# Linear attention beside an MLP: the second block pair's queries as chunk pairs of the seven-product loop

## The chip, the cores and the metric

The kernel runs on one core of a Trainium2 chip. The metric is the device time of one execution in microseconds (us), taken as the median of several runs; less is better.

## The reference

x is 2048 tokens by 512 channels, in float32. The kernel computes x + A(xn) + B(xn), where xn is x normalised over its channels:

```python
    qkv = (xn @ wqkv).reshape(B, S, 3, H, Dh)          # 32 heads of 16 channels
    phi = lambda t: jnp.where(t > 0, t + 1, jnp.exp(t)) + 1e-6
    pq, pk = phi(q), phi(k)
    kv = jnp.einsum("bhsd,bhse->bhde", pk, v)
    z = jnp.einsum("bhsd->bhd", pk)
    num = jnp.einsum("bhqd,bhde->bhqe", pq, kv)
    den = jnp.einsum("bhqd,bhd->bhq", pq, z)[..., None] + 1e-6
    A = (num / den) @ wo                               # heads side by side again
    h = relu(xn @ w1 + b1); B = (h * h) @ w2 + b2      # 1376 hidden features
```

## The kernel before, in words

TensorE takes its operands as rounded float32 (F32R). To keep accuracy, every operand is split into a high and a low part, and a product is three matmuls: high by high, high by low, low by high (`three`, L126). `split` (L116) makes the parts: ACT copies the high part out, DVE (or POOL) subtracts it for the low part.

The 2048 tokens are 16 tiles of 128 and four blocks of 512 (numbers 3, 2, 1, 0). The kernel goes over the tiles once for the keys and the sums of pk by xn (L693 to L736); then it goes over two pairs of blocks, blocks 3 and 2 with n = 0, blocks 1 and 0 with n = 1 (L837). x1 and x2 hold the two blocks' normalised tokens by channels, high and low parts; the tokens of blocks 1 and 0 wait in DRAM (xTd) until the first pair is done.

For each pair:

- *Queries* (`queries`, L404): one projection for each of the eight token tiles, 12 matmuls each, with tokens on the partitions; then phi (L368: ACT Relu, ACT Exp, DVE combine). For the second pair all eight stand at the start (L892 to L905), with the sums and the first weight splits between them.
- *Attention* (`attention`, L412): five DVE instructions for a token tile: multiply with z (zb, on all partitions), reduce over each head's 16 channels, add 1e-6, reciprocal, multiply. The denominators lie along the free dimension, so tokens stay on the partitions. `regroup_q` (L427) moves the finished 128-token tiles by DMA so that `attention_T` (L441) can turn them by 32x32 transposes on DVE to channels on the partitions, then makes high and low parts (aT). These are the stationary operands of `add_attention` (L509), whose moving operand m is the key-value matrix by wo.
- *The seven-product loop* (L970): the hidden features go in 11 chunks of 128; the last chunk, with 96, is done plainly (`plain_1`, L479). The other ten are five chunk pairs. A pair of chunks by two token blocks by two halves of the channels is a two by two by two product; it is computed with seven products instead of eight (the scheme of Strassen and Winograd). Each product (`product`, L485) is six matmuls of 128x512. The weights' sums S1 to S4 (`chunk_sums`, L743; splits into aop, L752 to L758) are made one iteration ahead, the tokens' sums T1 to T4 (`sums_of`, L775) once for each pair of blocks. The order in an iteration is fixed by hand: A (A11), B (A12), C (S1), the former pair's A22, S2 into A's bank, S4 into C's, S3 into A's. Between them ACT copies banks out (c11, t5, c12), DVE adds the other bank (L992, L978, L1046), and ACT applies Relu with the bias. c12 is copied after S2 and before S3 adds into the same bank. MLP sums (`mlp_2`, L493: 12 matmuls) of the first block stand between the products; with two of them, an iteration has 66 matmuls.
- *Second half* (L1082 to L1172): the first block's attention sums and output, then the second block's: nine MLP sums (index e), its attention sums, and the last two features. Here `wait_for` makes the hidden parts of the second block, which lie in r2, and `w2next` the parts of the w2 rows, three sums ahead. For the first pair this half also loads the next pair's tokens (L1096, L1124) and splits them (columns_todo), and splits wq for the next queries (`piece_q`, L171).

The program order is written out by hand (`manual_schedule`): every engine and every DMA queue takes its instructions in the order of the code. Nearly all DMAs go through SP's queue. Buffers come from pools with tags: "p" and "raw" have six slots of 128x512, "pair" five; a tile's slot waits for the last reader of the one before. TensorE has eight banks of PSUM: four for the products ("ps"), four for the block's output sums ("acc").

Of the kernel before, what the change touches and what calls it, by code (L numbers as in the profile page):

```python
# [18 lines left out]
def kernel(  # L19
# [130 lines left out]
    zb = keep.tile([P, D], F32, name="zb")  # L150
    eps = keep.tile([P, 1], F32, name="eps")
# [357 lines left out]
    def add_attention(acc, i, last=False):  # L509
        t = aT.pop(i)  # L510
        for j in range(NJ):
            three(acc[i % TB], [t[:, u, j * P:(j + 1) * P] for u in range(2)],
                  [m[u][:, j, :] for u in range(2)], False, last and j == NJ - 1)
# [226 lines left out]
    def load_1(n):  # L740
        return [raw_1(2 * n + k).rearrange("p (c n) -> p c n", c=2) for k in range(2)]
# [95 lines left out]
    for n in range(2):  # L837
        t1, t2 = NB - 1 - 2 * n, NB - 2 - 2 * n
        x1, x2 = xsb
        tag = "acc" if n else "ps"  # L840
        if n:

            o34 = [halves(xT[t])[1] for t in (t2, t1)]
            sums = sums_of(xT[t1], xT[t2], *o34)
        z = pair(f"w1z{n}") if n else None

        def small_chunk():
            t = raw_1(NF - 1)
            return lambda: split(z[:, 0], z[:, 1], t, "act", "dve")

        def first_split():
# [5 lines left out]
        def second_split(s12, s34):  # L857
# [4 lines left out]
        at1 = [lambda k=k: attention(t1 * TB + k) for k in range(TB)] + [lambda t=t1: regroup_q(t)]  # L862
        at1 += [lambda k=k: attentions_T(t1 * TB + k, t1 * TB + k + 1) for k in (0, 2)]
        at2 = [lambda k=k: attention(t2 * TB + k) for k in range(TB)]


        if n == 0:
            do(sums)
            queries(t1 * TB + 2)
            zs = small_chunk()  # L870
            w = load_1(0)
# [3 lines left out]
            z = pair("w1z0")  # L875
# [4 lines left out]
            ss = first_split()  # L880
# [5 lines left out]
            second_split(*ss)  # L886
            w2next = piece_2(NF - 1, 0)
            matrix(2)
        else:
            zs = small_chunk()  # L890
            w = load_1(0)
            for k in range(TB):  # L892
                queries(t1 * TB + k, tag)
                if k == 0:
                    zs()
                else:
                    do(sums)
            for k in range(TB):
                queries(t2 * TB + k, tag)
                if k == 0:  # L900
                    do(sums)
                if k == 1:
                    ss = first_split()
                if k == 2:
                    second_split(*ss)  # L905
# [5 lines left out]
        w = load_1(1)  # L911
# [58 lines left out]
        for p in range(NP + 1):  # L970
            fa, fb = 2 * p, 2 * p + 1
# [3 lines left out]
            if p < NP:  # L975
# [5 lines left out]
            if 0 < p < NP:  # L981
                chunk_split(1, 0, s34)
            if p:
                relu(r2[fb - 2], t5, fb - 2)
            if p == 1:
                next_2(2)
            if p < NP:
# [3 lines left out]
                high_2()  # L991
                nc.vector.tensor_tensor(out=c11, in0=B, in1=c11, op=OP.add)  # L992
                relu(c11, c11, fa)
            if p < NP:
                next_2(2 * p + 1)
# [3 lines left out]
            if p == NP:  # L999
                attention_places(*(("r1", "r3") if n else ("r2", "r0")))  # L1000
                do(at1)
                mlp_2(acc, fa - 2, s.pop(fa - 2))
            if p:
                product(before, A22b, [T[4][:, u] for u in range(2)], False, True)
                c21 = w512(f"c21_{n}_{p}", "p", 6)
                relu(c21, before, fb - 2)
            if p == NP:
                break
            t5 = t5_
            if p == 0:  # L1010
                T.update({k: tokens_sum(k, f"B{k - 3}") for k in (3, 4)})
# [6 lines left out]
            if p or n:  # L1018
                do(at1 if p < TB else at2)
            if p:  # L1020
                s[fb - 2] = hidden_2(f"s{n}_{fb - 2}", c21)
                mlp_2(acc, fa - 2, s.pop(fa - 2))
            else:
# [5 lines left out]
            s[fa] = hidden_2(f"s{n}_{fa}", c11)  # L1029
            if p + 1 < NP:  # L1030
# [3 lines left out]
            if p + 2 < NP:  # L1034
                w = load_1(p + 2)
            if p == NP - 1:
# [4 lines left out]
            if p + 1 < NP:  # L1041
                chunk_split(0, 1, s12)
            if p == NP - 1:
                do(at2)
            product(C, S4, [x[:, 2:] for x in x2], False, True)
            nc.vector.tensor_tensor(out=c12, in0=C, in1=c12, op=OP.add)  # L1046
            high_2()
            if p == 0:
                last_sums(4, difference_high)
            relu(r2[fa], c12, fa)  # L1050
            if p:
                next_2(2 * p + 2)
                mlp_2(acc, fb - 2, s.pop(fb - 2))
            else:
                for k in range(TB):
                    last_2(acc[k], k, sz, True, False)
                quarters_2(acc, sz)
            if p == TB - 1:
                do(at1)
                move(16)  # L1060
            product(A, S3, [T[3][:, u] for u in range(2)])
            if p == 2:
                load_res(t1)
            if p == 3:
# [18 lines left out]
        s1 = hidden_2(f"s{n}_{f}", c21)  # L1083
        for g in waiting[4:9]:
# [116 lines left out]
```

## Time and profile before

| | |
|---|---|
| median of 3 runs | 421.85 us (421.46 to 422.19) |
| the profiled execution's own time | 422.41 us |
| its span, first to last instruction | 420.7 us |
| busy: PE, DVE, ACT, POOL | 414.1, 304.9, 253.0, 55.2 us |
| mean granted TensorE clock | 0.999 |
| HBM read, written | 37.23 MB, 8.91 MB |

Engines: PE is TensorE (PEld its weight loads, which overlap), DVE VectorE, ACT ScalarE, POOL GpSimd, SP SyncE, whose queue issues DMAs. A profile row of a group gives line, engine, operation, output<-input, shapes, count, then busy us and mean ns of one, then the idle time of the engine before them and what released it. Rows of the chain and of the timeline begin with the start and the duration in us. Matmul records are pipelined and overlap: of two that follow each other the distance of the starts is the pace, not the duration.

### The profile page before, as it was taken

Reading aid. Unit: us, or ns where it says so; the run is one execution under the profiler, and the core shown is the slowest. Engines: PE = TensorE matmul, PEld = TensorE weight load, DVE = VectorE, ACT = ScalarE, POOL = GpSimd, SP = SyncE. Lnnn points to the kernel's source line nnn. Section 1 sums busy time; section 2 is a strip of 40 time slices with the busy share of each in tenths; the row PEclk is TensorE's granted clock in tenths of the full one; section 3 lists DMA queues with packets and bytes.
Section 4 is the critical chain, followed back from the end, with each engine's and each line's share of the span. In section 5 each row is a group of like instructions: output and inputs, shape, how many; then the busy total and the mean of one; then the engine's idle time right before and its main releaser. Section 6 shows DMA issues by size and latency. Waiting matters only on the chain.

```text
span 420.7 us, 5470 instructions
## 1 busy us (share of the span) xinstructions
PE 414.1 (98%) x1859; PEld 340.6 (81%) x1859; DVE 304.9 (72%) x555; ACT 253.0 (60%) x451; POOL 55.2 (13%) x78
## 2 busy tenths in 40 slices
PE   7999999999999999999999999999999999999996
PEld 6788888888887788888888887888788888888875
DVE  5995767786679987777579397586977667577293
ACT  5767777675467777565466371666677665546140
POOL 3231222220004000110000061001000200000240
PEclk9999999999999999999999999999999999999999
DMA  6885423800511322695026676501121784023742
GB/s 235 274 234 163 130 92 99 277 25 3 125 50 52 99 64 63 191 184 175 0 69 190 192 230 159 139 0 50 44 82 26 225 172 153 2 94 87 193 77 100
DMA packets 49485, 50.69 MB, mean 120 GB/s; under 512 B 8241, under 2 KB 33585, under 8 KB 49202
## 3 DMA queue, kind: packets, MB, share of 16 engines
q1 hardware_dynamic: 47154, 46.16, 36.4%
q0 software_dynamic: 2304, 4.20, 6.1%
q8 instruction: 14, 0.23, 0.3%
q14 instruction: 13, 0.11, 0.1%
HBM read 37.23 MB, written 8.91 MB: 110 GB/s over the span
## 4 chain that ended last, share of the span: by engine, by line
PE 96%; DMA 2%; DVE 1%; SPq 1%; issue 0%
PE acc L129 36%; PE b L489 23%; PE kx L398 10%; PE pq L379 10%; PE pk L379 9%; PE acc L500 2%; DMA x<-in_A_x_dram 2%; PE pz L129 1%; PE b L129 1%; PE pkv L820 1%; PE pm L129 1%; PE pt L318 0%; PE acc L507 0%; SPq L527 0%; SPq L157 0%; PE end L129 0%
## 5 line engine op out<-in xcount | busy, mean ns | idle before, releaser
L129 PE MATMUL acc<-w2r,s 128*128 128x512 f32 x477 | 112.8, 389 | 0.0
L129 PEld LDWEIGHTS acc<-w2r,s 128*128 128x128 f32 x477 | 89.5, 188 | 18.9 <-issue 0.2
L489 PE MATMUL b<-T,aop 128*128 128x512 f32 x240 | 59.9, 390 | 0.0
L489 PEld LDWEIGHTS b<-T,aop 128*128 128x128 f32 x240 | 44.8, 188 | 9.8 <-issue 0.5
L398 PE MATMUL kx<-pk,tok 128*128 128x512 f32 x192 | 46.8, 393 | 0.0
L398 PEld LDWEIGHTS kx<-pk,tok 128*128 128x128 f32 x192 | 35.6, 188 | 8.0 <-DVE pk L387 0.6
L956 POOL DMA_DIRECT2D res<-in_B_b_dram x16 | 14.1, 1067 | 150.5 <-DMA res<-in_A_x_dram 57.5
L121 DVE TENSOR_TENSOR w2r<-r,w2r 128x512 fp32r<-128x512 f32 (+2 forms) x35 | 25.4, 725 | 7.3 <-ACT w2r L110 7.2
L129 PE MATMUL acc<-mh,aTsr 128*128 128x512 f32 x96 | 30.6, 391 | 0.0
L118 POOL TENSOR_TENSOR tok<-xp,tok 128x512 fp32r<-128x512 f32 x16 | 21.7, 1363 | 54.8 <-ACT tok L110 54.8
L110 ACT ACTIVATE w2r<-r 128x512 fp32r<-128x512 f32 x32 | 20.0, 625 | 13.7 <-PE acc L129 11.3
L489 PE MATMUL b<-xs0h,aop 128*128 128x512 f32 x80 | 26.4, 391 | 0.0
L118 DVE TENSOR_TENSOR s<-c,s 128x512 fp32r<-128x512 f32 x20 | 13.8, 692 | 15.0 <-ACT s L110 14.9
L110 ACT ACTIVATE aop<-S 128x512 fp32r<-128x512 f32 x20 | 12.6, 629 | 16.1 <-DVE S L749 12.3
L374 DVE SCALAR_TENSOR_TENSOR q<-pq,q 128x512 f32<-128x512 f32 x16 | 11.0, 690 | 14.4 <-ACT q L372 14.4
L129 PEld LDWEIGHTS acc<-mh,aTsr 128*128 128x128 f32 x96 | 18.0, 188 | 4.0 <-issue 0.2
L370 ACT ACTIVATE q<-pq 128x512 f32<-128x512 f32 x16 | 9.4, 590 | 18.6 <-PE pq L379 18.5
L129 PE MATMUL acc<-ml,aTsr 128*128 128x512 f32 x48 | 18.7, 390 | 0.0
L964 DVE TENSOR_TENSOR res<-acc,res 128x512 f32<-128x512 f32 x16 | 11.0, 692 | 9.9 <-PE acc L129 6.6
L489 PEld LDWEIGHTS b<-xs0h,aop 128*128 128x128 f32 x80 | 15.0, 188 | 3.4 <-ACT rz L477 0.3
L303 DVE STREAM_TRANSPOSE at<-g 128x512 f32<-128x512 f32 x16 | 10.4, 689 | 7.9 <-DMA g<-q 7.9
L489 PE MATMUL b<-xs0l,aop 128*128 128x512 f32 x40 | 15.6, 390 | 0.0
(208 smaller groups left out, 854.9 us busy)
## 6 DMA issues: line engine op xcount, KB each, us to landing
r<-in_B_w_dram SPq DMA_DIRECT2D x49, 256.0 KB, 3.1
res<-in_A_x_dram SPq DMA_DIRECT2D x8, 512.0 KB, 5.8
res<-in_B_b_dram POOLq DMA_DIRECT2D x16, 256.0 KB, 5.3
g<-q SPq DMA_DIRECT2D x64, 64.0 KB, 2.5
out_dram<-res SPq DMA_DIRECT2D x15, 256.0 KB, 2.1
x<-in_A_x_dram SPq DMA_DIRECT2D x5, 512.0 KB, 6.0
via<-xp SPq DMA_DIRECT2D x5, 512.0 KB, 2.7
xg<-via SPq DMA_DIRECT2D x20, 128.0 KB, 2.9
```

The costliest lines, as they stand in the source:

```text
L110: nc.scalar.activation(o, i, AF.Copy, bias=bias)
L118: ENG[el].tensor_tensor(out=l, in0=src, in1=f32(h), op=OP.subtract)
L121: nc.vector.tensor_tensor(out=l, in0=src, in1=f32(h), op=OP.subtract)
L129: nc.tensor.matmul(ps, lhsT=a[u], rhs=b[v], start=first and n == 0, stop=last and n == 2)
L303: nc.vector.transpose(o.rearrange("p j (r t) -> p r j t", r=NJ), G.rearrange("p r (j c) -> p r j c", j=NJ))
L370: nc.scalar.activation(p, ps, AF.Relu, scale=-1.0)
L374: nc.vector.scalar_tensor_tensor(p, ps, 0.0, p, op0=OP.max, op1=OP.add)
L379: nc.tensor.matmul(ps, lhsT=cols(i)[u][:, j, slot(i)], rhs=w[v][:, j, :], start=first and n == 0, stop=last and n == len(steps) - 1)
L398: nc.tensor.matmul(kxp[c], lhsT=tok[i][:, u, c * P:(c + 1) * P], rhs=pk[i][:, v], start=i == 0 and (u, v) == first, stop=i == NT - 1 and ( ...
L489: nc.tensor.matmul(ps, lhsT=a[u][:, j * P:(j + 1) * P], rhs=b[v][:, j, :], start=first and j == 0 and n == 0, stop=last and j == 1 and n == 2,
L956: nc.gpsimd.dma_start(r[:, i], b2[None, :].partition_broadcast(P), accum_op=OP.add)
L964: nc.vector.tensor_tensor(out=r[:, a:z], in0=ps, in1=r[:, a:z], op=OP.add)
```

## The change

The second pair of blocks no longer projects its queries tile by tile. wq's 512 columns are treated as four more chunks of 128, two more chunk pairs of the loop, which for n = 1 runs over seven pairs in the order q, w, q, w, w, w, w. A query chunk comes out with channels on the partitions and 512 tokens along the free dimension, for both blocks, which is the layout that `add_attention` wants; so `regroup_q` and the turns go for this pair. The eight results (two blocks, four chunks) are called units here. The denominators need a sum over channels, now the partitions: `steps_of` weights the unit by z on ACT (a scale and a bias for each partition, from zc), turns the result in 32x32 blocks on DVE, reduces over each head's 16 channels, takes the reciprocal, and turns the quotients back with a read that repeats each one 16 times.

```diff
+    def phi_T(o, src):
+        e = w512("phi", "p", 6)
+        nc.scalar.activation(e, src, AF.Relu, scale=-1.0)
+        nc.scalar.activation(e, e, AF.Exp, scale=-1.0)
+        nc.vector.scalar_tensor_tensor(o, src, 0.0, e, op0=OP.max, op1=OP.add)
+
+    def steps_of(t, j, done=False, parts=False):
+        o = q[t][:, j]
+        tiles = []
+        blocks = lambda ap: ap.rearrange("p (r c) -> p r c", c=32)
+        heads_of = lambda ap: ap.rearrange("p (h d) -> p h d", h=H)
+        by_heads = lambda ap: ap.rearrange("p (r h) d -> p r h d", h=2)
+        def weighted():
+            pz = w512(f"pz{t}_{j}", "p", 6)
+            tiles.append(pz)
+            nc.scalar.activation(pz, o, AF.Identity, bias=zc[:, 1, j:j + 1], scale=zc[:, 0, j:j + 1])
+        def sums():
+            pt = w512(f"pt{t}_{j}", "p", 6)
+            den = small.tile([P, H], F32, name=f"dt{t}_{j}", tag="den")
+            nc.vector.transpose(blocks(pt), blocks(tiles[0]))
+            nc.vector.tensor_reduce(den, heads_of(pt), axis=AX.X, op=OP.add)
+            tiles.append(den)
+        def quotients():
+            pz, den = tiles
+            nc.vector.tensor_scalar(den, den, 1e-6, None, op0=OP.add)
+            nc.vector.reciprocal(den, den)
+            nc.vector.transpose(by_heads(heads_of(pz)), by_heads(den[:, :, None].to_broadcast([P, H, D // H])))
+        def divide():
+            nc.vector.scalar_tensor_tensor(o, o, 1e-6, tiles[0], op0=OP.add, op1=OP.mult)
+        def into_parts():
+            a = aT[t, j] = places.pop(0)
+            split(a[:, 0], a[:, 1], o, "act", "dve")
+        return [lambda: phi_T(o, o)][done:] + [weighted, sums, quotients, divide] + [into_parts][:parts]
...
+    def raw_q(f):
+        t = w512(f"rq_{f}", "raw", 6)
+        nc.sync.dma_start(t.rearrange("p (j n) -> p j n", j=NJ),
+                          wqkv[:, f * P:(f + 1) * P].rearrange("(j p) n -> p j n", j=NJ))
+        return t
...
+    def z_columns():
+        of_g = zd.rearrange("o (g j c) -> g c (o j)", g=NJ, j=NJ)
+        for g in range(NJ):
+            nc.sync.dma_start(zc[32 * g:32 * (g + 1), 0], of_g[g])
+        return lambda: nc.vector.tensor_scalar(zc[:, 1], zc[:, 0], 1e-6, None, op0=OP.mult)
...
+        order = [("w", k) for k in range(NP)]
         if n:
+            order[:1] = ("q", 0), ("w", 0), ("q", 1)
+        NO = len(order)
+        AT = ((0, 0, 0, 0, 0, 0, 0, 0, 0),
+              (0, 0, 0, 0, 1, 1, 0, 0, 0),
+              (2, 0, 0, 0, 1, 1, 0, 1, 0),
+              (2, 0, 0, 1, 1, 0, 1, 0, 1),
+              (2, 0, 1, 0, 0, 0, 1, 0, 1),
+              (0, 1, 0, 0, 0, 0, 0, 1, 0),
+              (1, 2, 1, 0, 0, 0, 2, 0, 0),
+              (1, 0, 1, 0, 1, 1, 0, 2, 3))
+        AE = (2, 1, 4, 2, 1, 3, 1, 7, 2, 3, 1)
```

AT says how many steps of the units are issued at each of nine places of an iteration (places in the order 7, 0, 1, 8, 2, 3, 4, 5, 6; `step` takes the first block's steps first), AE how many beside each MLP sum of the second half. In the loop:

```diff
-            if p:
-                nc.vector.tensor_tensor(out=t5, in0=before, in1=t5, op=OP.add)
+            if was:
+                nc.vector.tensor_tensor(out=t5 if was == "w" else q[t2][:, pb], in0=before, in1=t5, op=OP.add)
...
-                nc.vector.tensor_tensor(out=c11, in0=B, in1=c11, op=OP.add)
-                relu(c11, c11, fa)
+                nc.vector.tensor_tensor(out=c11 if kind == "w" else q[t1][:, fa], in0=B, in1=c11, op=OP.add)
+                if kind == "w":
+                    relu(c11, c11, fa)
+                else:
+                    steps[t1] += steps_of(t1, fa, parts=True)
...
+                else:
+                    phi_T(q[t1][:, pb], before)
+                    steps[t1] += steps_of(t1, pb, True, True)
...
-            if p == NP - 1:
+            if p > 1:
                 do(at2)
+            step(at_p[4])
             product(C, S4, [x[:, 2:] for x in x2], False, True)
...
+            def second_sums(f=pb, first=not was):
+                if first:
+                    for k in range(TB):
+                        last_2(acc[k], k, sz, True, False)
+                    quarters_2(acc, sz)
+                else:
+                    mlp_2(acc, f, s.pop(f))
+            if kind == "q":
+                put_off = second_sums
+            elif was != "q":
+                second_sums()
...
             product(A, S3, [T[3][:, u] for u in range(2)])
```

A put-off sum is issued in the next iteration, after the former pair's A22. `do(at2)` (an attention of the second block, n = 0) thus also stands in the third and fourth iterations. The z columns are loaded in the first pair's third iteration. For n = 1 the eight `queries` calls are gone: the small chunk's product follows the first pair's last sums at once.

The first pair's second half takes over what stood among the second pair's queries, and drops wq's pieces; both token loads move ahead of the w2 pieces:

```diff
+        prepare = []
+        if n == 0:
+            f1, f2 = (keep.tile([P, NJ, BT], F32, name=f"xT{t}", tag=f"xT{k}") for t, k in ((t1 - 2, t1), (t2 - 2, t2)))
+            nc.sync.dma_start(f1, xTd[t1 - 2])
+            nc.sync.dma_start(f2, xTd[t2 - 2])
+            o34 = halves(four("Tf1", "r0"))
...
+            prepare = [lambda x=x, f=f, j=j: columns(x, f, j) for j in range(NJ) for x, f in ((x1, f1), (x2, f2))]
+            prepare[6:6] = sums_of(f1, f2, *o34)[:2]
+            prepare += sums_of(f1, f2, *o34)[2:]
         for g in waiting[4:9]:
             w2next.extend(piece_2(g, place(g)))
...
+            do(prepare, 2 if e < 6 else 1)
+            if n == 0:
+                if e == 4:
+                    z = pair("w1z1")
+                    zs = small_chunk(z)
+                if e == 5:
+                    w = load_1("q", 0)
+                if e == 7:
+                    zs()
...
+            else:
+                step(AE[e])
+        if n:
+            step(len(steps[t2]))
+            do(parts_2, NJ)
         for k in range(TB):
...
+            if n == 0:
+                if k == 0:
+                    ss = first_split(w)
+                if k == 2:
+                    second_split(w, *ss)
```

The first query chunk's splits are thus made beside the first pair's last attention sums. The five hidden chunk pairs, the MLP sums and the attention sums (their operand now cut from four units) stay as they were.

More of the change, by code (lines that the diff above doesn't have):

```diff
@@ L509, in add_attention @@
     def add_attention(acc, i, last=False):
-        t = aT.pop(i)
+        b, k = i // TB, i % TB
+        t = aT.pop(i, None)
         for j in range(NJ):
-            three(acc[i % TB], [t[:, u, j * P:(j + 1) * P] for u in range(2)],
-                  [m[u][:, j, :] for u in range(2)], False, last and j == NJ - 1)
+            a = [t[:, u, j * P:(j + 1) * P] if t is not None else aT[b, j][:, u, k * P:(k + 1) * P] for u in range(2)]
+            three(acc[k], a, [m[u][:, j, :] for u in range(2)], False, last and j == NJ - 1)
     pw = bank("warm")
@@ L889 @@
         else:
[L890 to L905, printed above, removed]
             w2next = []
@@ L968, in store, with step @@
             nc.sync.dma_start(of[i * P:(i + 1) * P, a:z], res[t, k][:, a:z])
-        for p in range(NP + 1):
-            fa, fb = 2 * p, 2 * p + 1
+        def step(k=1):
+            for _ in range(k if n else 0):
+                do(steps[t1] or steps[t2])
+        for p in range(NO + 1):
+            at_p = AT[p]
+            kind, k = order[p] if p < NO else ("", 0)
+            fa, fb = 2 * k, 2 * k + 1
+            was, k = order[p - 1] if p else ("", 0)
+            pa, pb = 2 * k, 2 * k + 1
             A, before, B, C = banks[p % 2], banks[(p + 1) % 2], *banks[2:]
```

181 lines of the change are left out of this document (96 added, 85 removed).

## The prediction

> **What bounds the kernel now.** I read the page first (span, busy shares, chain), then the chain in order of time, then stages.
>
> ```profile
> span 420.7 us, 5470 instructions
> PE 414.1 (98%) x1859; PEld 340.6 (81%) x1859; DVE 304.9 (72%) x555; ACT 253.0 (60%) x451; POOL 55.2 (13%) x78
> PE 96%; DMA 2%; DVE 1%; SPq 1%; issue 0%
> ```
>
> A busy PE alone proves little, since its records overlap; the chain proves it, 96% of it being PE. Next, that chain where the second pair of blocks starts.
>
> ```profile
> 261.00 21.76 PE pq L379 x96
> 282.76 2.72 PE pz L129 x12
> 285.48 4.08 PE b L489 x18
> ```
>
> Start, duration, count: each piece begins where the last ends. A matmul takes 21.76/96 = 0.2267 us, and so it does in the seven products (4.08/18).
>
> ```profile
> core 0: us, PE busy (x) PEld busy (x) DVE busy (x) ACT busy (x) POOL busy (x), PEclk, DMA share, GB/s
> 156.37:171.33 14.96, 14.96 (x67) 12.39 (x67) 11.57 (x22) 10.45 (x18) 0.00 (x0) 1.00 0.30 85
> 206.70:261.00 54.30, 54.30 (x241) 44.40 (x241) 40.32 (x65) 28.89 (x50) 8.83 (x10) 1.00 0.55 155
> 261.00:362.77 101.77, 101.77 (x452) 83.83 (x451) 74.65 (x136) 63.96 (x110) 4.62 (x5) 1.00 0.36 96
> 362.77:420.70 57.93, 54.41 (x245) 44.46 (x244) 34.69 (x56) 22.65 (x38) 7.79 (x10) 1.00 0.38 100
> ```
>
> The rows are a chunk pair of the first loop, the first pair's second half (two blocks finished after the loop), the second pair's queries and loop, and its second half. PE busy equals the length everywhere but at the end, at full clock: no PE stall is left to win back. Only fewer matmuls shorten this kernel, and any new wait of PE lengthens it one for one.
>
> **What is removed on PE.** Eight query projections of twelve matmuls (x96 above) go. Two chunk pairs come, each seven products of six: 84. The small chunk's products, the MLP sums and the attention sums keep their counts. So 12 matmuls go: 12 x 0.2267 = 2.72 us. The Trainium skill, "TensorE: Matmul & The Clock Gate", section "Wait — 56ns, not 53.3ns?", gives a 512-column matmul 215.7 ns when warm; by it the saving would be 2.59 us. The row disagrees, and the row decides.
>
> **What is added beside PE.** Durations:
>
> ```profile
> L303 DVE STREAM_TRANSPOSE at<-g 128x512 f32<-128x512 f32 x16 | 10.4, 689 | 7.9 <-DMA g<-q 7.9
> L418 DVE TENSOR_REDUCE den<-pz 128x32 f32<-128x512 f32 x16 | 11.0, 686 | 0.6
> L420 DVE RECIPROCAL den<-den 128x32 f32<-128x32 f32 x16 | 5.7, 353 | 0.6
> L118 DVE TENSOR_TENSOR aop<-S,aop 128x512 fp32r<-128x512 f32 x20 | 13.7, 687 | 0.2
> L749 DVE TENSOR_TENSOR S<-S,r 128x256 f32<-128x256 f32 x10 | 4.3, 425 | 0.3
> L110 ACT ACTIVATE aop<-S 128x512 fp32r<-128x512 f32 x20 | 12.6, 629 | 16.1 <-DVE S L749 12.3
> L372 ACT ACTIVATE q<-q 128x512 f32<-128x512 f32 x16 | 10.1, 633 | 0.5
> L261 ACT ACTIVATE xp<-x,y 128x512 f32<-128x512 f32 x8 | 6.0, 802 | 0.0
> ```
>
> A new unit is one block's 128 query channels by 512 tokens; there are eight. On DVE: phi 0.69, transpose 0.69, reduce 0.69, add about 0.18 (an estimate: half the reciprocal of the same shape), reciprocal 0.35, transpose back 0.69, divide 0.69, low part 0.69: 4.67 us. On ACT: two steps of phi at most 1.27 (L372 is the second), the weighting with per-channel scale and bias 0.80 (L261 has such operands), high part 0.63: 2.7 us. The transpose back reads a stride of zero, which no row shows: 0.69 if it streams like L303, at most 1.38 if each element costs twice; I take 0.69, the same instruction. At 1.38 the eight units add 5.5 us of DVE. An old tile cost nearly the same DVE (phi 0.69, attention 2.6, turn 0.69, low part 0.7), and 1.9 us of ACT.
>
> In the stage 261.00 to 362.77 DVE loses the sums for T1..T4 (12 x 0.69), the small chunk's 0.69, six attentions (6 x 2.6), phi of two later units (1.4), four turns and low parts (2.8); it gains one chunk pair's splits and sums (3 x 0.69 + 0.42 + 4 x 0.42 = 4.2), six additions for the query products (4.1), and the steps of the first block's four units and one of the second's (4 x 3.98 + 3.3). 74.65 - 28.7 + 27.5 = 73.5 us of 99. ACT gains one pair's splits (3 x 0.63 + 0.4), six bank copies (3.8), five weightings (4.0) and four high parts (2.5), and loses four copies of the sums, the small chunk's, two turned tiles' and phi of two units (4 x 0.63 + 0.6 + 1.3 + 2.5): 63.96 + 12.6 - 6.9 = 69.7 of 99. Neither becomes the bound by its sum; order inside the stage decides.
>
> The second half of the second pair gets 14 steps and four part pairs for two attentions, turns and their waits on moved data: about 34.69 + 5 of 55 us. The steps end by the seventh MLP sum, the parts (4 x 0.63 ACT, 4 x 0.69 DVE) run beside the last two sums, 5.44 us of PE. Cost taken: 0; without that cover, 2.8 us.
>
> **The loop, where PE has least slack.** One iteration of the second loop:
>
> ```profile
> 319.08 2.88 PE L129 MATMUL acc<-w2r,s 128*128 128x512 f32 x12
> 319.29 0.69 ACT L477 ACTIVATE c<-b,b1s 128x512 f32<-128x512 f32 x1 [0.71 <-PE b L489]
> ...
> 322.46 0.92 ACT L110 ACTIVATE aop<-r 128x512 fp32r<-128x512 f32 x2
> 323.36 0.60 ACT L110 ACTIVATE c<-b 128x512 f32<-128x512 f32 x1
> 324.52 1.75 PE L129 MATMUL acc<-w2r,s 128*128 128x512 f32 x7
> ```
>
> At 323.36 ACT copies the S2 product out (c12), the moment it exists; the S3 product adds into that bank and must wait for it. Now an MLP sum of 12 (2.72 us) stands between. The change puts that sum off in the query chunk pairs, and the pair behind each has none at that place: four times only S4's six matmuls, 1.36 us, cover the copy's 0.60. ACT may come some 0.7 us late; each further us is a PE us. It came here after 4.07 us of work (319.29 to 323.36): a relu 0.72, two hidden chunks' squares and copies, two splits 0.90, so a hidden chunk is (4.07 - 0.72 - 0.90)/2 = 1.2. New work at that place: behind a query pair phi's two steps 1.27, one hidden chunk 1.2, splits 0.9, once a high part 0.6: 3.4 to 4.0 us; in the second query pair relu 0.7, hidden 1.2, splits 0.9: 2.8. In the first, the small chunk's relu (0.69) and two splits start only when its product ends, six matmuls before S2 does: 0.69 + 0.9 and 0.21 from PE's end to ACT's start (319.08, 319.29) against 1.36, about 0.45 us late, 0.3 to spare. So: 0 to 0.3 us.
>
> ```profile
> 221.63 0.68 DVE L417 SCALAR_TENSOR_TENSOR pz<-q,zb 128x512 f32<-128x512 f32 x1
> ...
> 224.29 0.68 DVE L118 TENSOR_TENSOR s<-r2a,s 128x512 fp32r<-128x512 f32 x1
> 224.89 0.68 DVE L118 TENSOR_TENSOR s<-r2b,s 128x512 fp32r<-128x512 f32 x1
> ```
>
> DVE's instructions start 0.60 apart when nothing holds them (224.29 to 224.89), and an attention takes 2.66 (221.63 to 224.29). DVE is fullest in the fourth pair: eleven instructions of 512 columns 6.6, transpose and reduce 1.4, quotients 1.3, last split and sums 2.1: 11.4 of 54 x 0.2267 = 12.24 us. Its deadline for PE (the addition before A22) lies 18 matmuls, 4.1 us, behind its release. Cost taken: 0; if the broadcast transpose doubles, the pair is at 12.1, still 0.
>
> **In the first loop** the second block's attentions move forward: one more (2.66 us) in the third and fourth iterations, while the fifth keeps its two. 11.57 + 2.6 = 14.2 of 14.96: full, but the same addition is then about 1.3 us later, with 4.1 to spend. Cost 0.
>
> **The first pair's second half, the other narrow place:**
>
> ```profile
> 217.47 27.41 PE L129 MATMUL acc<-w2r,s 128*128 128x512 f32 x120
> 244.71 0.40 PE L129 MATMUL acc<-mh,aTsra 128*128 128x512 f32 x1
> ```
>
> ```profile
> 241.46 1.30 DVE L303 STREAM_TRANSPOSE at<-g 128x512 f32<-128x512 f32 x2 [3.36 <-DMA g<-q]
> ...
> 247.21 1.94 DVE L121 TENSOR_TENSOR aTsr<-at,aTsr 128x512 fp32r<-128x512 f32 x2
> ```
>
> PE's rows first, then DVE's. Two attentions leave DVE here (L417 at 221.63 is one's start), four query splits (2.7) too; sums (8.3), small chunk (0.7) and the first query chunk's splits and sums (4.2) come: 40.32 + 5.2 = 45.5 of 54.3. Walking DVE's queue: the third MLP sum ends at 217.47 + 48 x 0.2267 = 228.4, which frees the place that ACT's next copy (0.63) waits for, so DVE goes on near 229.3. For the next three sums it has 8, 4 and 8 instructions (hidden low part, w2 low part, and six for T or two columns): 20 x 0.60 and some 0.6 of waits between dependent ones, until 241.9. One w2 low part is ahead of the turns, which start near 242.5 instead of 241.46. The moves leave 2.7 us earlier (no attention at 221.63 before them), so DMA no longer ends that wait; DVE does. The first low part is ready near 244.5, needed at 244.71 + 2 x 0.2267 = 245.2; the third tile's near 249.4, needed near 250.6. Margins 0.6 and 1.2 us: cost 0, with 1 us possible. If a doubtful term takes more, PE waits for the rest.
>
> ```profile
> 190.95 2.92 SPq L163 DMA_DIRECT2D r<-in_B_w_dram  x6
> 217.66 0.33 SPq L1096 DMA_DIRECT2D xt<-xTd  x1
> ```
>
> SP now meets both 1 MB token loads before five w2 pieces, and waits until the last product frees aop at 206.7, where this stage begins. The pieces left at 190.95; now they follow 2 MB:
>
> ```profile
> xt<-xTd SPq DMA_DIRECT2D x2, 1024.0 KB, 5.3
> b1s<-in_B_b_dram SPq DMA_DIRECT2D x1, 5.0 KB, 3.4
> ```
>
> 206.7 + 2 x 5.3 + 1.3 = 218.6 for the first, 1.3 us apart; it is wanted after the first MLP sum, 217.47 + 24 x 0.2267 = 222.9. Covered, at worst by 4 us. The 2 KB of z by channels go as 512 single numbers in four DMAs; the 5 KB of b1 of that kind landed in 3.4 us, and these have over 100 us, the DVE product that waits for them stands an iteration (15 us) behind. The loop's query weights replace as many bytes of wq.
>
> **Sum.** 422.41 (the profiled execution: span 420.7 and 1.7 around it) - 2.72 + 0.3 = 420.0; from the median 421.85 the same step gives **419.4 us**.
>
> **Rivals.** (1) *DVE late in the first pair's second half.* For: the margin of 0.6 us, and the low parts at 247.21 take 1.94 for two beside POOL's copies. Against: the two attentions that leave. 2.8 us more DVE there makes 2.2 us of waits: 421.3. (2) *The c12 copy comes late in the four pairs without cushion.* For: ACT already arrives just in time at 323.36. Against: the counts above are smaller than 4.07. It decides from 0.7 us late; 2 us late each costs 4 x 1.3 = 5.2 us: 424.3, slower. (3) *The change doesn't do what it says*: the 12 matmuls are gone by count, so only waits can eat them; that they eat all in many small pieces gives 421.9.
>
> **Chances.** Forecast 0.66; (1) 0.14; (2) 0.14; (3) 0.06. What a measurement here can tell from no change is about 0.2%, 0.84 us. Faster: 0.66 and a third of (1), 0.71. Same: the rest of (1), a third of (3), 0.11. Slower 0.18. The range goes from no wait at all less the spread of the runs, 418.8, to 421.9, past rival 1 (the forecast's own cases end at 420.3, the possible 1 us above); above it lie (2) and half of (3).
>
> **What will show it.** Right: PE about 1847 matmuls, PE busy near 411.4, the chain without DVE or ACT in the middle; 84 more under the product line, 96 fewer under the projections. Wrong: PE waiting for ACT c12 before an S3 product (rival 2), for DVE's low part of aT near 245 to 250 (rival 1), a transpose row near 1.4 us, a w2 copy waiting for its DMA after 223.

## The result, and the profile after

The changed kernel takes **418.46 us** (median of 6 runs, 418.24 to 418.49) where the kernel before took 421.90 in the same session; the ratio is 0.9912, 95% interval [0.9895, 0.9929]. That is faster, as forecast, and it lies 0.34 us below the lower end of the range (418.8). The profiled execution took 418.24 us.

First the page of the kernel after: span, busy times, and the chain by engine.

```profile
span 416.5 us, 5454 instructions
PE 410.9 (99%) x1847; PEld 338.5 (81%) x1847; DVE 313.1 (75%) x574; ACT 262.0 (63%) x469; POOL 56.4 (14%) x78
PE 98%; DVE 1%; DMA 1%; ACT 0%; issue 0%
```

1847 matmuls instead of 1859, and 98% of the chain is PE's. (So it is in e1, a second profile of the kernel before, below; the 96% ahead of the change belonged to an execution that started late.) The chain in order of time, where the second pair of blocks starts (start, duration, what, count):

```profile
259.99 2.72 PE pz L129 x12
262.71 4.08 PE b L533 x18
266.79 2.72 PE b L129 x12
269.51 9.52 PE b L533 x42
279.03 1.81 PE acc L544 x8
```

The 21.76 us of projections are gone. The loop starts with the small chunk, each piece begins where the last ends, and a matmul still takes 9.52/42 = 0.2267 us. The stages of the kernel after, as they were shown for the one before:

```profile
core 0: us, PE busy (x) PEld busy (x) DVE busy (x) ACT busy (x) POOL busy (x), PEclk, DMA share, GB/s
205.80:259.99 54.19, 54.19 (x242) 44.42 (x241) 44.20 (x72) 31.30 (x55) 8.52 (x10) 1.00 0.58 175
259.99:359.03 99.04, 99.04 (x440) 81.58 (x439) 73.26 (x135) 67.86 (x118) 4.62 (x5) 1.00 0.35 91
359.03:416.50 57.47, 54.23 (x245) 44.47 (x244) 35.30 (x58) 25.48 (x43) 9.32 (x10) 1.00 0.29 83
```

PE is busy for the whole of the first two stages. A busy PE alone proves little, so here are all the waits of PE that the profile of the kernel after lists (us in total, times, longest):

```profile
PE pt L319 <- DVE y L253: 1.3, 1, 1.3
PE warm L566 <- PEq L1315: 0.8, 1, 0.8
PE pk L380 <- ACT xs1h L335: 0.3, 1, 0.3
```

All three lie in the first 7.5 us, and the kernel before has them too: the change brings no new wait. The middle stage shrank from 101.77 to 99.04 us, by 2.73, which is the 12 matmuls. The neighbours shrank too, by 0.11 (from 54.30) and 0.46 us (from 57.93), and that the prediction did not have.

The new operations, by the groups of the kernel after (busy us, mean ns of one, idle time before):

```profile
L484 DVE STREAM_TRANSPOSE pz<-dt 128x512 f32<-128x512 f32 x8 | 5.7, 711 | 0.3
L476 DVE STREAM_TRANSPOSE pt<-pz 128x512 f32<-128x512 f32 x8 | 5.6, 705 | 0.9 <-ACT pz L471 0.9
L487 DVE SCALAR_TENSOR_TENSOR q<-q,pz 128x512 f32<-128x512 f32 x8 | 5.5, 685 | 0.1
L471 ACT ACTIVATE pz<-q,zc 128x512 f32<-128x512 f32 x8 | 6.4, 805 | 1.0 <-DVE q L457 1.0
```

The transpose that reads a stride of zero (L484) takes 711 ns: it streams like the other one. The weighting takes 805 ns against the 802 of the row it was taken from.

**Where the rest of the gain is.** Distances between the same matmuls in the traces, in us; the mean of two profiled executions of each kernel (of the kernel before: that of the prediction and e1; of the kernel after: that of this section and e2), which differ by 0.05 at most:

| from, to | before | after | difference |
|---|---|---|---|
| first kx sum to the first of the seven products (n = 0) | 111.70 | 111.64 | -0.06 |
| to the second pair's start | 131.85 | 131.75 | -0.10 |
| to the quarter sums (L507, L551) of the last block | 148.25 | 145.39 | -2.86 |
| to the end of the last matmul | 8.10 | 8.04 | -0.06 |
| to the end of the span | 3.50 | 3.28 | -0.22 |

The third line holds the 12 matmuls (2.72) and 0.14 more. So 0.35 us (from the unrounded distances) is spread over all stages, also those that the change doesn't touch, and 0.22 us lies behind the last matmul. The 0.35 us is not a quicker pace of every matmul. Most starts lie some 227 ns apart in both kernels, but from the first kx sum on 145 and 135 of them (the two executions of the kernel before) come 230 to 245 ns behind the one ahead, against 88 and 87 in the kernel after; what these starts take beyond 226.7 ns falls from 0.96 and 0.89 us to 0.54 and 0.54. What comes ahead of the first kx sum varies from run to run: it starts at 16.4 to 17.3 us in these four executions (the profile of before that the prediction used was the late one), and at 18.2 us in e5's.

Behind the last matmul only the last store is left. The stretches of the kernel before, then of the kernel after; both begin 0.46 us after the last matmul, and the DMA share is the last column but one:

```profile
417.64:419.20 1.56, 0.00 (x0) 0.00 (x0) 0.01 (x1) 0.00 (x0) 0.00 (x0) 1.00 0.94 327
419.20:420.69 1.49, 0.00 (x0) 0.00 (x0) 0.00 (x0) 0.00 (x0) 0.00 (x0) 0.83 0.00 0
```

```profile
413.72:415.28 1.56, 0.00 (x0) 0.00 (x0) 0.00 (x1) 0.00 (x0) 0.00 (x0) 1.00 0.93 326
415.28:416.54 1.26, 0.00 (x0) 0.00 (x0) 0.00 (x0) 0.00 (x0) 0.00 (x0) 1.00 0.00 0
```

In both the data is out about 2.02 us after the last matmul; what differs is the time in which nothing moves, 1.49 against 1.26 us. In the trace SP waits there for the eight semaphores of its transfers (counters that tell of their landing), one after the other. The times of these waits, in us after the last matmul, by the semaphores' numbers (read from the traces' instructions):

```
                102   103   104   105   106   108   109   110   next
before          0.99  1.63  2.03  2.38  2.44  2.50  2.56  2.62  2.68
after           0.98  1.04  1.11  1.17  1.23  1.62  2.00  2.39  2.46
e5 (after + 1)  2.39  2.45  2.52  2.58  2.64  2.70  2.76  2.82
```

The transfers take these semaphores in turn. In the kernel before, the last store happened to be on 105, and four waits of 0.06 us came behind its landing; SP issues 220 transfers there and 192 after the change, and with 192, a multiple of eight, the last store is on 110, the last to be waited for. That is a reading; e5, e6, e9 and e10 tested it.

### The profile page after: what moved, and what is told of

Same layout as the page of the kernel before. It is cut to its first block, busy times and chain, and to the rows that moved or that the text cites. A ratio compares the mean times of both kernels' runs of the same rounds, so it can differ in the third digit from the quotient of the medians.

```text
span 416.5 us, 5454 instructions
## 1 busy us (share of the span) xinstructions
PE 410.9 (99%) x1847; PEld 338.5 (81%) x1847; DVE 313.1 (75%) x574; ACT 262.0 (63%) x469; POOL 56.4 (14%) x78
## 4 chain that ended last, share of the span: by engine, by line
PE 98%; DVE 1%; DMA 1%; ACT 0%; issue 0%
PE acc L129 37%; PE b L533 28%; PE kx L399 11%; PE pk L380 11%; PE pq L380 5%; PE acc L544 2%; PE b L129 1%; PE pz L129 1%; PE pkv L880 1%; PE pm L129 1%; DMA x<-in_A_x_dram 1%; PE pt L319 1%; PE acc L551 0%; DVE st L233 0%; PE end L129 0%; DVE xp L272 0%
## 5 line engine op out<-in xcount | busy, mean ns | idle before, releaser
L533 PE MATMUL b<-T,aop 128*128 128x512 f32 x288 | 71.8, 390 | 0.0
L533 PEld LDWEIGHTS b<-T,aop 128*128 128x128 f32 x288 | 53.8, 188 | 11.7 <-issue 0.2
L129 PE MATMUL acc<-mh,aTsr 128*128 128x512 f32 x112 | 35.4, 390 | 0.0
L533 PE MATMUL b<-xs0h,aop 128*128 128x512 f32 x96 | 31.7, 390 | 0.0
L129 PEld LDWEIGHTS acc<-mh,aTsr 128*128 128x128 f32 x112 | 21.0, 188 | 4.6 <-issue 0.2
L129 PE MATMUL acc<-ml,aTsr 128*128 128x512 f32 x56 | 21.8, 389 | 0.0
L118 DVE TENSOR_TENSOR aop<-S,aop 128x512 fp32r<-128x512 f32 x24 | 16.9, 706 | 3.5 <-ACT aop L110 3.1
L533 PE MATMUL b<-xs0l,aop 128*128 128x512 f32 x48 | 18.7, 389 | 0.0
L533 PE MATMUL b<-xs1h,aop 128*128 128x512 f32 x48 | 16.7, 389 | 0.0
L110 ACT ACTIVATE c<-b 128x512 f32<-128x512 f32 x24 | 14.1, 588 | 3.5 <-PE b L533 3.3
```

The costliest lines, as they stand in the source:

```text
L110: nc.scalar.activation(o, i, AF.Copy, bias=bias)
L118: ENG[el].tensor_tensor(out=l, in0=src, in1=f32(h), op=OP.subtract)
L129: nc.tensor.matmul(ps, lhsT=a[u], rhs=b[v], start=first and n == 0, stop=last and n == 2)
L533: nc.tensor.matmul(ps, lhsT=a[u][:, j * P:(j + 1) * P], rhs=b[v][:, j, :], start=first and j == 0 and n == 0, stop=last and j == 1 and n == 2,
```

## The experiments

Each was timed beside the kernel before on the same chip. The kernel before took 421.78 us beside e1 to e4, 421.67 beside e5 to e8, and 421.80 beside e9 to e12.

### e1 to e4: is it the 12 matmuls?

e1 and e2 are the two kernels again. e3 shortens three of the second pair's projections of the kernel before, e4 does one product of the kernel after twice:

```diff
-                queries(t1 * TB + k, tag)
+                queries(t1 * TB + k, tag, HL[:-4] if k < 3 else HL)
```

```diff
     plain_1(ps, z, x1)
+    if n:
+        plain_1(ps, z, x1)
```

> The kernel before, unchanged, on the chip that also runs the next three. Theory A (the change took exactly the 12 matmuls, 2.72 us; the 0.7 us beyond them is the service of DMAs at both ends, where the third x tile and the last store landed sooner in the profile after): its own start varies, so the first kx matmul may come anywhere from 16.4 to 17.5 us, and the time moves with it, 421.0 to 422.5. Theory B (the change itself makes the start quicker): the first kx again near 17.4 us and the time near 421.9.

> The kernel after, unchanged, on the same chip. Theory A: paired with the kernel before it is 2.7 us quicker, ratio 0.9936, and its first kx is as early or as late as that of e1. Theory B: 3.4 us quicker, ratio 0.992, first kx near 16.5 us whatever e1 shows.

> The kernel before without the last four matmuls (low part of the tokens by the high part of wq) of three of the second pair's eight query projections: 12 matmuls are left out, nothing else. Theory A: 2.72 us less than e1, and the same time as e2 within 0.3. Theory B: 2.72 less than e1, but 0.7 more than e2.

> The kernel after with the small chunk's product for the first block of the second pair done twice (the second start overwrites the first), 12 matmuls more, so PE has the count of before. Theory A: 2.72 us above e2, equal to e1 within 0.3. Theory B: 2.72 above e2 and 0.7 below e1.

Measured: e1 421.86 (ratio 1.0002 [0.9992, 1.0011]), e2 418.53 (0.9930 [0.9919, 0.9942]), e3 420.58 (0.9971 [0.9961, 0.9981]), e4 421.04 us (0.9983 [0.9974, 0.9991]). e2's interval holds the ratios of both theories; e4 decides. With its 12 matmuls back the changed kernel is 2.51 us slower in the medians (2.77 in the profiles, from the first kx sum to the last matmul) and still 0.74 faster than before, and its slowest run (421.44) is quicker than the quickest of the kernel before beside it (421.62): the excess is real, which theory A did not allow. It does not sit where theory B put it, in the start: the first kx comes at 16.63 us in e1 and at 16.71 in e2.

e3 missed in the other direction: the same 12 matmuls taken out of the kernel before bring 1.2 us, not 2.7. Its waits of PE (us in total, times, longest):

```profile
PE b L489 <- DVE c L1046: 0.4, 1, 0.4
PE pk L379 <- ACT xs1h L334: 0.3, 1, 0.3
PE b L489 <- DVE aop L118: 0.3, 1, 0.3
```

The first and the third are new, both in the first two chunk pairs of the second pair's loop, for VectorE's results. From start to start, with the slow starts behind them, they cost PE 0.66 and 0.52 us, and a third place between them 0.07: 1.25 of the 1.33 us by which that stretch (second pair's start to quarter sums, 146.86 us) stays above 148.25 - 2.72. The kernel before had no reserve beside PE just there. So the gain of 2.72 is not the count alone; the change also leaves the work beside PE where PE doesn't ask for it too early.

### e5, e6, e9, e10: the closing waits

To one kernel or the other some transfers of 32 bytes are added that nobody reads, right behind the load of z; `n` is 1, 4 and 8 on the kernel after (e5, e9, e10), 4 on the kernel before (e6):

```diff
     nc.sync.dma_start(zb, zd.partition_broadcast(P))
+    more = keep.tile([1, 8 * n], F32, name="more")
+    for k in range(n):
+        nc.sync.dma_start(more[:, 8 * k:8 * (k + 1)], zd[:, 8 * k:8 * (k + 1)])
```

> The kernel after, with one more transfer of 32 bytes that nobody reads, issued by SP right behind the load of z over all partitions, in the middle of the kernel. Theory A (closing waits): SP's transfers take eight semaphores in turn, and SP ends the kernel by waiting for these eight one after the other, about 0.06 us apart. In the kernel before the last store sits on the fourth of them, so four waits stand behind its landing; in the kernel after it sits on the last. One more transfer moves the last store to the first one: the packets of the last store end where they did, about 2.0 us after the last matmul, but seven waits come behind it, so the span grows by 7 x 0.06 = 0.4 us, from 416.8 to 417.2, and the time from 418.5 to 418.9-419.0. Theory B (the last store itself is served quicker in the kernel after, by the smaller number of transfers or other addresses): one transfer more changes nothing, 418.5, and the last matmul to the span's end stays 3.28 us.

> The kernel before, with four more transfers of 32 bytes that nobody reads, at the same place. Theory A (closing waits): the last store moves from the fourth to the eighth semaphore, the four waits behind it go, and from the last matmul to the span's end it takes 3.27 us instead of 3.50: the time falls by 0.23 us, from 421.8 to 421.6, although there is more to do. Theory B (quicker service of the store itself): nothing changes or it is slower, 421.8 to 422.0, and the distance stays 3.50.

> The kernel after, with four more transfers of 32 bytes that nobody reads. Theory A (closing waits, by the number of SP's transfers modulo eight): the last store comes to the fourth semaphore, where the kernel before has it; four waits of 0.06 us stand behind it, from the last matmul to the span's end it takes 3.50 us instead of 3.28, and the time is 418.5 + 0.23 = 418.75 us. If the small change of matmul pace that the runs with other counts showed (a mean distance of 227.2 ns in the kernel before and 227.0 in the one after, 227.1 with one transfer more) hangs on the count too, another 0.2 to 0.3: 419.0 us, as far above the kernel after as that kernel's gain exceeded its 12 matmuls. Theory B (one transfer more cost 0.4 for another reason, as SP being held up): four cost more than one, above 419.3.

> The kernel after, with eight more transfers of 32 bytes that nobody reads. Theory A (closing waits, by the number modulo eight): the last store is back on the last semaphore, 3.28 us from the last matmul to the end, 418.5 us, less than with one or four transfers more. Theory B (each transfer costs by itself): the slowest of the three, above 419.5.

| | last store on | last matmul to end | first kx to last matmul | median us |
|---|---|---|---|---|
| kernel before (e1) | 105 | 3.50 | 399.87 | 421.86 |
| e6, before + 4 | 110 | 3.24 | 399.73 | 421.31 |
| kernel after (e2) | 110 | 3.28 | 396.83 | 418.53 |
| e5, after + 1 | 102 | 3.71 | 397.18 | 419.19 |
| e9, after + 4 | 105 | 3.52 | 396.76 | 418.62 |
| e10, after + 8 | 110 | 3.28 | 397.45 | 418.50 |

The column from the last matmul to the end decides: with every count (193, 196 and 200 transfers of SP on the kernel after, 224 on the kernel before) the end is as theory A has it, to within 0.03 us, and behind its last matmul the kernel before ends sooner with four transfers more. The times alone would not show that: e6 and the kernel before beside it can't be told apart (ratio 0.9993 [0.9985, 1.0002]). The medians follow less exactly, because the matmuls' pace changes as well: one small transfer (e5) costs 0.34 us ahead of the last matmul, spread over all stages, and four cost nothing there. So the pace that came with the change is no property of its parts either; the small edit of e5 takes nearly all of it away again, and has 132 of the starts of 230 to 245 ns, where e9 has 63. Two executions of one kernel have them nearly all at the same matmuls (behind 100 us, 112 of 115 and 113 in the kernel before, 57 of 59 and 63 in the one after), so they belong to the program and not to the run. The edit adds a transfer, and also a tile of 32 bytes on one partition, which may move the tiles placed behind it; the traces hold no addresses, and no run tells the two apart. (e10's profiled execution has one wait of 0.55 us at 137.9 us, in a stage that the change doesn't touch; its median has no such loss.) What sets the pace stays open.

### e7 and e12: the c12 copy (rival 2)

First the profile after at the four places: ScalarE's c12 copies in the first four chunk pairs of the second loop, with their idle time and its cause in brackets.

```profile
270.97 0.59 ACT L110 ACTIVATE c<-b 128x512 f32<-128x512 f32 x1
...
282.90 0.60 ACT L110 ACTIVATE c<-b 128x512 f32<-128x512 f32 x1 [0.49 <-PE b L533]
...
295.14 0.60 ACT L110 ACTIVATE c<-b 128x512 f32<-128x512 f32 x1 [1.17 <-PE b L533]
...
307.38 0.60 ACT L110 ACTIVATE c<-b 128x512 f32<-128x512 f32 x1 [0.16 <-PE b L533]
```

ScalarE is there ahead of PE in three of them, and just in time in the first. e7 makes it late:

```diff
+            for _ in range(4 if n and p < 4 else 0):
+                copy("act", c12, zb)
             copy("act", c12, A)
```

> The kernel after, with four needless ScalarE copies (zb into the place of c12, some 0.60 us each, 2.4 together) right ahead of the c12 copy in the four chunk pairs that have no MLP sum between S2 and S3. It puts rival 2 of the prediction to the test, with its decision point of 0.7 us. In the profile after, ScalarE waits 0, 0.49, 1.17 and 0.16 us for PE at these four places, so the copies make it 2.4, 1.9, 1.2 and 2.2 us late. By the prediction's point: 1.7 + 1.2 + 0.5 + 1.5 = 4.9 us of PE waits, 423.4 us, all of them ahead of the S3 products. The other theory (the place has more cushion than 1.36 us, or ScalarE's lateness is partly taken back by the idle time behind it before PE asks): under 2.5 us, below 421.

Measured: 425.41 us (1.0101 [1.0085, 1.0117]), 6.9 us more than the kernel after (e2); 4.9 were expected. PE's waits and, in the first of the four places, ScalarE's copies:

```profile
PE b L533 <- ACT c L110: 5.8, 4, 2.0
```

```profile
271.04 2.60 ACT L110 ACTIVATE c<-zb 128x512 f32<-128x512 f32 x4
273.67 0.60 ACT L110 ACTIVATE c<-b 128x512 f32<-128x512 f32 x1
```

The copies delayed the real one by 2.63 us, not 2.4. With the idle times above it was 2.6, 2.1, 1.5 and 2.5 us late, and the matmuls stood still for 2.18, 1.48, 0.87 and 1.87 us: the place forgives 0.45 to 0.66 us, where the prediction had 0.7. The four stops sum to 6.40 us, and some 0.1 us for each restart brings that to the 6.9 measured. The mechanism is the one the prediction named.

e12 takes the put-off sum back into the query pair:

```diff
-            else:
-                put_off()
...
-            if kind == "q":
-                put_off = second_sums
-            elif was != "q":
+            if was != "q":
                 second_sums()
```

> The kernel after, with the MLP sum that a query pair puts off done in the query pair itself, between S4 and S3; the pair behind then has no MLP sum at all. All else and the number of matmuls stay. Theory A (no engine beside PE is near its limit there, so the order is free): no change, 418.5 us. Theory B (the sum put off is the time in which VectorE and ScalarE do the following pair's work): that pair falls from 12.2 us of PE work to 9.5 us, while VectorE has 10.0 us to do in the second and 10.8 in the fourth, so PE waits about 0.5 and 1.3 us in these two: 420 to 420.5 us, with waits for VectorE or ScalarE in the second and fourth pairs.

Measured: 422.37 us (1.0022 [1.0010, 1.0035]), 3.8 us more than the kernel after (e2) and slower than the kernel before; about twice what theory B expected. PE's waits, and ScalarE ahead of the c12 copy in the second chunk pair:

```profile
PE b L533 <- ACT c L110: 2.9, 2, 1.8
```

```profile
281.77 0.60 ACT L455 ACTIVATE phi<-b 128x512 f32<-128x512 f32 x1 [0.78 <-PE b L533]
282.40 0.64 ACT L456 ACTIVATE phi<-phi 128x512 f32<-128x512 f32 x1
282.94 0.62 ACT L497 ACTIVATE c<-c 128x512 f32<-128x512 f32 x1
283.58 0.63 ACT L110 ACTIVATE s<-c 128x512 fp32r<-128x512 f32 x1
284.12 0.92 ACT L110 ACTIVATE aop<-rq 128x512 fp32r<-128x512 f32 x2
284.95 0.57 ACT L110 ACTIVATE c<-b 128x512 f32<-128x512 f32 x1
```

This is the list that the prediction wrote down: phi's two steps, a hidden chunk, two splits, then c12. They start when A22's product ends (281.77), and without the sum of 2.72 us between that product and S2 the copy comes 1.9 us later than S2's end allows: PE stands still for 1.35 us here and 1.93 in the fourth pair. The sum that is put off does not only leave the S3 products without cushion; it is the time in which ScalarE does the query pair's work.

### e8: VectorE late in the first pair's second half (rival 1)

```diff
                 if e == 5:
                     w = load_1("q", 0)
+                    more = w512("more", "p", 6)
+                    for _ in range(4):
+                        nc.vector.tensor_tensor(out=more, in0=zb, in1=zb, op=OP.add)
```

> The kernel after, with four needless VectorE additions of 128x512 (some 0.60 us from start to start, 2.4 together) in the first pair's second half, behind the fifth of its MLP sums' splits. It puts rival 1 of the prediction to the test: VectorE is on time there with a margin that the prediction put at 0.6 us for the first two turned tiles and 1.2 us for the third; in the profile after the turns start 0.26 us earlier than forecast and the first low part stands about 1.2 us ahead of the matmul that reads it. If the margin is 1.2: PE waits about 1.2 us at that stage's attention sums, 419.7 us. If it is 0.6 as predicted: 1.8 us, 420.3. If VectorE's idle time in the stage takes all of it: 418.5, no wait.

Measured: 420.27 us (0.9966 [0.9954, 0.9979]), 1.74 more than the kernel after. By the number alone that is the margin of 0.6. The trace says otherwise: VectorE of the kernel after, then of e8.

```profile
240.84 1.30 DVE L304 STREAM_TRANSPOSE at<-g 128x512 f32<-128x512 f32 x2
242.24 1.30 DVE L121 TENSOR_TENSOR aTsra<-at,aTsra 128x512 fp32r<-128x512 f32 x2
```

```profile
240.41 2.87 DVE L1260 TENSOR_TENSOR more<-zb 128x512 f32<-128x512 f32 x4
243.19 0.68 DVE L121 TENSOR_TENSOR w2r<-r,w2r 128x512 fp32r<-128x512 f32 x1
243.80 1.30 DVE L304 STREAM_TRANSPOSE at<-g 128x512 f32<-128x512 f32 x2
245.20 1.29 DVE L121 TENSOR_TENSOR aTsra<-at,aTsra 128x512 fp32r<-128x512 f32 x2
```

The four additions took 240.41 to 243.19, 2.78 us and not 2.4 (they write the same tile and start 0.70 apart). PE stopped for 1.31 us before the first attention matmul, for ScalarE's high part, and for another 0.17 two matmuls on, for the low part; with some 0.1 us that each restart costs it is 1.58 us up to the low part. 2.78 - 1.58 = 1.2: the margin is the one read from the profile after, twice the predicted one. The first to be late is the high part, which the prediction left out; by 2.78 - 1.31 it has about 1.5 us to spare.

### e11: the broadcast transpose twice

```diff
             nc.vector.reciprocal(den, den)
+            for _ in range(2):
                 nc.vector.transpose(by_heads(heads_of(pz)), by_heads(den[:, :, None].to_broadcast([P, H, D // H])))
```

> The kernel after, with each of the eight broadcast transposes done twice, 0.71 us more of VectorE for each unit, 5.7 in all. It tests the prediction's statement that the changed loop would hide even a transpose of twice the price. VectorE is busy for 7.4, 10.0, 10.7 and 10.8 of about 12 us in the first four chunk pairs after. Theory A (the prediction): no new wait of PE, 418.5 us. The other theory (the fullest pair has no room for two more such instructions, since their place matters and not the sum): PE waits 0.3 to 1.5 us, 418.8 to 420.

Measured: 420.11 us (0.9960 [0.9948, 0.9973]), 1.6 more than the kernel after. Neither theory holds: there is a wait, but not in the fullest pair of the loop. PE's one new wait, and its place:

```profile
PE acc L129 <- DVE aTsr L118: 0.9, 1, 0.9
```

```profile
398.82 0.74 PE L129 MATMUL acc<-mh,aTsr 128*128 128x512 f32 x2 [0.91 <-DVE aTsr L118]
```

None is in the loop, where the prediction had worked out that even the double price fits (fourth pair at 12.1 of 12.24 us): right. It is in the second pair's second half, which the prediction priced at 0 by its sum and by a cover of two MLP sums. A stretch of the kernel after shows how thin that cover is:

```profile
390.00:398.00 8.00, 8.00 (x37) 6.63 (x36) 7.83 (x11) 5.02 (x9) 5.23 (x6) 1.00 0.17 30
```

VectorE is busy for 7.83 of 8.00 us there, in a stage whose share is 35.30 of 57.47.

## Why the prediction was right, and where it was wrong

**PE is the bound, and the count is the saving: right.** 1847 matmuls as counted, PE busy 410.9 (411.4 was forecast), 12 x 0.2267 = 2.72 in the stage that loses them, measured 2.73 in the profile and 2.51 us by putting them back (e4). By the Trainium skill's figure that stands beside it there ("TensorE: Matmul & The Clock Gate", section "Wait — 56ns, not 53.3ns?") it would have been 2.59; in the trace the distance of the starts stayed 0.2267.

**The added work: right in size.** VectorE 73.26 against 73.5 and ScalarE 67.86 against 69.7 us in the middle stage, VectorE 44.20 against 45.5 in the first pair's second half. Only the second pair's second half was off: 35.30 instead of about 39.7; why is not worked out here. The one price that no row showed, the broadcast transpose, was taken at 0.69 and is 0.711.

**The waits: right, for the reasons given.** The c12 copy came in time four times (lateness 0 against "0 to 0.3"), and its point of decision is 0.45 to 0.66 us late instead of 0.7. VectorE's turns in the first pair's second half had 1.2 us to spare instead of 0.6. Both rivals are true mechanisms at the places named (e7, e8); neither was reached. In e12 rival 2 makes the same change slower than the kernel before.

**The failed step is the sum:** "422.41 - 2.72 + 0.3", and behind it the lower end, "no wait at all less the spread of the runs, 418.8". It held that beside the count only new waits could move the time, so that nothing but the spread of the runs lay beyond a gain of 2.72. In place of the +0.3 came 0, as its own walk had found; and two terms that it put at nothing, without a reason, came on the other side: 0.22 us from SP's closing waits, since the number of transfers changed, and 0.35 us from matmul starts of 230 to 245 ns that became fewer. 421.85 - 2.72 - 0.22 - 0.35 = 418.56, against 418.46 measured; so 0.87 of the 0.94 us by which the forecast was too high have their place. The cause of the first is shown (e5, e6, e9, e10), and its sign is luck: 192 transfers happen to be a multiple of eight. The second is measured, and its cause stays open.

## What to carry to other kernels

Where PE's chain is unbroken, count its matmuls, and then ask at each place how late each neighbour may be: here 0.5 us for ScalarE at one place and 1.2 for VectorE at another, in stages where their busy times (67.86 of 99.04 us, 44.20 of 54.19) promised far more. Taking matmuls out alone brought 1.2 of 2.7 us (e3), and the same change with one sum in another order lost (e12); the order of the work beside PE is what lets a saving arrive. When a forecast is worth tenths of a microsecond, look behind the last instruction as well, and let the range allow for what any rebuilt program may shift.

## What the runs showed of the hardware

- SP's closing waits cost 0.06 us each behind the last store's landing: from the last matmul to the end it took 3.24 to 3.71 us, by the number of SP's transfers modulo eight (220 and 196: 3.50 and 3.52 us; 193: 3.71; 192, 200 and 224: 3.28, 3.28 and 3.24).
- A wait of PE of some 2 us can be followed by a stretch at half the clock. In e7's profiled execution eight matmuls soon after the first wait (2.18 us) started 0.427 us apart instead of 0.227, with the granted clock at 0.61 in the mean of the stretch:

```profile
274.10:278.40 4.30, 4.08 (x11) 3.28 (x12) 3.02 (x5) 2.36 (x5) 0.00 (x0) 0.61 0.23 65
```

  That is 1.6 us; e7's runs lie at 425.3 to 425.4 (three) and 426.9 (two), and of e12's 11 runs four lie at 423.7 to 424.0, the others at 422.1 to 422.4. The longer runs have a granted clock of 0.996, the others 0.999 to 1.000. That the waits bring it is not shown: the kernel before, beside e1 to e4, has two runs of 38 (423.40 and 423.63 us) with a clock of 0.995 and no wait over 1.6 us in any profile. The Trainium skill, "TensorE: Matmul & The Clock Gate", section "Part 1: The HAM clock gate (the "warmup" mystery)", has the clock halved after an idle window of about 3.4 us, with a window that runs freely. The halved clock and its length of 3.4 us (8 x 0.427) agree with this run; the wait ahead of it was shorter, 2.18 us.
- The mean distance of the matmuls' starts changes by 0.1% between programs that differ in one transfer of 32 bytes and its tile (396.83 and 397.18 us from the first kx sum to the last matmul, e2 and e5), through the number of starts that come 230 to 245 ns apart instead of 227. Nothing in the rows shows why.
